# Weights in halves at the start, a store in halves at the end, and a new order between them, in a two-layer attention and feed-forward kernel

**Chip, cores, metric.** One core of one Trainium2 chip. The metric is the device time of one execution in microseconds (us); most quoted times are medians of six executions. The time before is 567.18 us, the median of three executions (565.27 to 567.36).

## The reference, cut to what matters

Four residual steps on x of 2048 x 640: memory attention (four segments of 512 tokens, 32 heads of 20), feed-forward (640 to 1728 to 640), and both again.

```
x = x + A(layernorm(x));  x = x + B(layernorm(x))      # and the same two once more
A: q, k, v = x@wq, x@wk, x@wv                          # 32 heads, width 20
   for s in range(4):                                  # segments of 512 tokens
       p = softmax(q_s k_s' * scale + mask)
       o_s = g * phi(q_s)M / (phi(q_s)z + 1e-6) + (1-g) * p v_s      # g = sigmoid(beta)
       M += phi(k_s)' v_s;  z += sum(phi(k_s))
   out = concat(o) @ wo
B: relu(x @ w1) @ w2
```

## The kernel before

The kernel is a planner. Streams (loads, layernorm, q and k, v, scores, apply, feed-forward, and so on) yield operations, each with the engines that may run it and the buffers that it takes; a table gives every operation a rank, and a list scheduler places them. The result is one fixed order for each engine. Those orders are what runs.

The profile calls TensorE PE, VectorE DVE, ScalarE ACT, GpSimd POOL, and SyncE, which issues transfers, SP. A *chain* of matmuls is a few of them that add up in one bank of PSUM, the memory that matmuls write; another engine must copy the bank out (*evict* it) before the kernel uses it again. The *chain* of the profile is something else: the work that ended last, followed back from wait to wait. A *mode change* is a step between matmuls that use the full array and matmuls on row or column tiles of it.

```
def loads_sp():                              # SyncE's queue
    for i in (0, 2):
        yield from x0("sp", i)               # x tiles 0 and 2, 160 KB each
    yield from ld("sp", "wv", 819200, lambda e: e.dma_start(wv_r[:], w_src(A_wv)), ("wv",))
    ... wk, wq alike
def loads_act():                             # ScalarE's queue
    for i in (1, 3):
        yield from x0("act", i)
    ...
def proj_v(a, s):
    wt = yield Need("wv")
    ...
    for i in range(NJ):                      # 4 x tiles
        for hf in range(2):                  # column halves: one chain of 5 matmuls each
            for k in range(FC): ...          # 128 x 320
...
def store(i):
    r0 = yield Need("xB", b, s, i, 0)
    r1 = yield Need("xB", b, s, i, 1)        # both halves of the last add
    to = yield dma("sp", dout[i], 163840, ...)
```

Ahead of the first v matmul, TensorE runs 14 warming matmuls of 512 columns and some filling ones of 128. Segment 0 then goes: v chains and q and k chains, evictions, scores, exponentials on ScalarE, apply.

The softmax here doesn't subtract the row's maximum and nothing guards it: scores larger than these inputs give would overflow.

Of the kernel before, what the change touches and what calls it, by code (L numbers as in the profile page):

```python
# [11 lines left out]
ALU = mybir.AluOpType  # L12

T = 2048
D = 640
# [399 lines left out]
c-  # L415
n1R3$UbBaqjcK=AZZ6xpVK_yZ5p8?t595eYq@;1$JR!c?v{8kw79EETSf2qA4q(QWdQz<Y6UPL9HYtWYIEZV#TCVR5YmslLBKBtPm=ZQV~UwW!
b&UF6`cC=j-pB`DZR=P0i!~&pF+Fy8Cp0-T!QJd!-~dOIb4cp<XB>@?J?Lk+12nRPfp^Z^36-
UeV1`#rGSypWwAwuExCEu&N@lJfj!m>MChq&ZIo4TS4<CjBJ+U`m|nv8F$Jzbr<H$;q$a!Cv|B_j@29Sz67hLr6b?g2jri0w=8Q-
y0WNiG4>X$ZDBl?{h+x?YBCBc-`6qlIRpw05-;e449SI<)xc{}_d(8W5`jkp?<vgMi8~I|w&43byd&)6a?pD_=%w<a-
YW;>eC%pW{!^!LZx`m;tZ{HGLkBr%tIlI58P@wf@5WeL4uk$MMxV!?a`~b@g8Q%N>yRji>_(*|-  # L420
_aZJYa4#GF*66%A*{>6C&G9IGG2_|b<mvGtD%Qo_*KR1??UHJcF;Bs``U)PdnwC`e)Pm1?0>&p3)}6IJ#q#3z7y|jWvd*N3t*XD@(%3jR?N9w*
2x{<u@|zx8+*J5JNgjxcNlZu4SqMtFUsAxelK=(6=r=zHsJT2Shqp01OMyg98fwecj4FhptT?RJomLjkm?`d4J-
O#@GU_PpIba6PwS#ONc%^yV$R)NApfR&u+xavO0hTCES|uQGii!>nb~auBP~!F0-Xui@?p6K-
eVSN<CS5ojNb{ZKMD<g3u{wIa#&{Nlx~DnZS15C9!*fGgK7@X*o^n}@>y`mWG!|wfwk-KYYo2bl?U!s_}h9=eFA)HSib>&If>cl;{Gu1bwG6ss
LwzXyCB{Bu%d!>LzufBJhsYN?Sfhhv`yxVAc1+sTGB7!eN?w&b_aWJ;ob)B$ziXf@+$O{z`M4Bb4+hYq0<sprSzXBR*!)87&yHIeVaeV;O*oaJ
XtAb=J>YvR?N=jIo$$n*WfXm<PY^{aWBGq0-
qVR?_~X43!ia#C!Argm}lGJmkW0y`e<)%k3z)XahTVmYIkD!W4(_f{g;haIHR}LQ?GzmG{DVfrSO{!+K8~L1$t5$r=r49lWq~3Q8oRnsOc$|`!
O;aXg-4Lt4K?+W?5Cu!foo^d~Z6)>7_C*_FXRcyYShYWplEyM?b?X6^D5yOG3I);2HBXDQGpqu6x&c&{Pucoz-
%<7tvy8)a$}zPYe6l{2J({ytZ#IOLdh@#&uYZ@Ol|CoP)V5n(#WOm)N(BlsIBkY~?VmR)#F&xMO>ofd_T)t4wYs+<i@_@p}lXUWQG~PmjUh%`O
S7^gUhD1+^%Z1!=vNGg*T6-p~d(wm`pvxjp$!_X+)cNqas};eJdfQDKLzh@J_gTc$7kSSLZ%RxRsE9i_ZEuN_Z<l75AL5e-  # L430
<;_L+l|r(^Sa8tYrm>$gS!^EU9SM=&oVl^iF~@qCx%4<re8bcIi+)J%`_DQ&K@V5QKC_mCX2N8!B1!N1*4IVJPRhP^R=Z@WCJy%{c0&%!zF-
;bonB__w7kN0)!cd()^=pbTrj<|C0oJ0l9SjvUZxgc{c5fMWi&cEMHGT`}Hpq~|IBO)C?K8Ep9Sf@Hf8ed|@H$SO{`F3}S7BY=B3jJvCp8o!tg
`T2;y~e?UCV?_?BwSr8ex;1NZa{Wd_)tPVt%9m6?A3dh26R6-?gr+&fid?}#`>?A5g-
c@B_iJN6vwEE>VU5dA!FE_^##`w<9WjPGaGE?<QH%!#oT`MPKr3~BSv4oI`tHT&b&se_8P6yKvbLnhZxZc(R3bKtiLIu#;f$vw^_U@{zn6vU(K
m+MSGPBy9{dEBaCQO{&F}ijy|}g=0T+pzk6$H!DmxwHUctjQh%>$CFsG?w*I8X#U3L>vYc@wLd>osE=`3o$830!{CCJ=r!kt4hw3upltrr)>&+
TV;PVpXX@_{&+hr5fESj1R*cmX5zN(IK&D$=O*F#+JuQ{!T$Q47PO4#$VdXFw+2MMT@Lqy3aX&L-
2&m`eI$E0s7Kd*Oi{UXoCB4{r$V)~UaaLbR>#}uRKb-
m0TGzZRHFX!3!&H9y9v8Oh0x?B;3E3(L4dfIVe|DMg<svI4?=}sg*f~AGW`t@lMnG$+u6mo^n9xjYUj4yrKClQPMUCS_S=)Z><T#+*zqeuUq*Z
PWP%rk~UmzXclhPY>T8j%-t9ak@CDRA=|j=9p?U^zr3&+%)>u#F($Qa}b3*f|SX%V*k@+-3`HCBY_++1_i!<SK>J?xUx_TM2l|5qa3!Qt-
)T)LO^j+b3}~gIcMJ`bPDA@{qm)uQxg`0%tDj_jSFzUmjCK1Ygyo`g8J>-YI{AN=Ws;^dTV8am@NPxnJk>S^YhE0=%BXno-nFcgx51wEn654)p  # L440
9$jXc1!G_OAZDn8AeKc~+C<(Gqg%|8}_Tuy7x1I`AFIOxSOHE|9;pVu>*2mSTVX~ffaT7Aw_jf%{4R{iNXixc*GutOE=hOje_kUnzkI%ci&SQA
g<H0(hoWfemmuM%R3;r}-3vK!?mh$%DB(<~yjMVGhXuGMfgyjyr>j6FGC4ZNpfL;J(Hw-xg<R4YFtpL88mEL&KoSaoPs(#x)i&ni|9qgENF9N%
-7U_}Fz%iuQzYIS*jZk+M5MGTvSeMYO|jbk)3zvznh>2iSr1~Xa`GEtd1cqN>cQqa4N-b5sj(~s-H23GZ&MbZIO;sVmJc#?z@*o)gqxT-
LcdKpUL<YfbSBf*|`NK(Z9nE2DOcn`Uq2~pgmlRj>b0yekU)F}{7{Y|+eCGCILi+H`L`->QPexR5H{F8=V`Bm)!DqcI0^rM-tHWKD=7siqTcU9
sV>A3+U=vW0NMXi>HeC08$=Q35qIWM7~TMbcUN#hXXmvshynBmM>RJzBllQdxEtU&J>z0_9@GeK{0K<14%<>#N^Oqa;F#EwhPyZUiGE9~<)xb@
|agO$^OC@mwVq+~I<#5@qO7WTAi)ZGd!I#kqAQP8d{>d8Ki_>9|06crOMd+(~P!d$)%@fu#ztk{|P>j~{+WYa{o$O`jnCv`#lo^Kj{Y|f&Vga6
+y*UNj5|98u;%H3FJU6?E78o2_pd}1+|<9a!CavC(hO}&~7Ejg-
=vB_iU8hkUB@2aouO)Fh|e_bO+7xVG|!TV9IvWL=wm8_5QTWY<g68P)`x3YXpV|E~F>{w;IZc^XZ$Q_t>J$UUwgqy?;ty5z$wG&RR>C!ZQ5cmH
AQEd-&vRl0uR+-
T&j55oRp~}eBmA#PR@8Txr)@A!jj(Bwh(JPZ{xu2>$sYmn?%4eOiR4$FIpEV=LR?HF?GM?J~CUJH`>$Wj_2FUils3x00_eU$^lwpXS!;~GtRK|  # L450
&XwqWj7yw^u-*e5)`QbA;{GlotuI=rTvC1<y!0V)UZedMI-SxMbp(RI<T=x^M?`I5X<OYGS==<P6O{wDM`&f0VbyKld(W+Cen9T4k<K14g!Fyo
+1L@n?hlEctto0*_a6qYmg+BrWY&%lm*vCEsII{P&n)v9|tg)QvCDwI0>t4_a*aZ(Rq)y}8^FB+C}S)(16e^JxC_sdkOtS&cz+X2kq99884(Av
-Q<fQj$*0;{8X>AhoE&$ixkE|a$CY$t_?w~h$+vc=DgVr+L?Zn!nu!D8k?xnno0i*S5CVx&1>)wdb=YfA??m2}vy7Enp>6;nG_RAMEWkk0w=*#
-JTA!<f>sfi%tDjGH$DfKGjJ_NlaHH<+b0+l@#L8EY+djN6k_YLbb$W^AkTSGnC*@YguL@&JD^z@jpRaV5OU^ReWZ;|9+kc>+#_9ZPZ7`O1#Ln
MF#()no7L4%zFe~UG+T-cSu?t|`>l28jR;5`d?{}#IZ|4g8cH5XEu5s3dEb+{)5TQ-
7=lBWiswTfdAFndc)#zc5Qjc}Ug*IjPXa0+*FlO2NTrb~ZH1E<zlXJ`3aMpR5W$)q^%&E(zq3?7X`;&&r*MYuawOc@Ml4rOMpU#-
^NANw4S5tPfub2@fKTa)LCK!f)T#T!K)f>RGi`PE(+-t-iWxP!GF>oHn7$Q%!9U5!O<;cHwPOXc34(RS<*EM1XKMVb+Q8`~eDc3<aHQ27k4ps-
WW-z{oQqE$YsKx#D?qQ6XpWMe-K1J)ACT7^hZ$pv;pftiWXU`s{SuMYH?$cN`#QyP6h}jWOO&1#bAY-DTz8ujz3OTlh_XF_!wbWc5D(HyyvsGq
y(K^$Ng0I5^;?Uul*Si>BtP5S1R=}W5)?XGcCZRcdn$ZMh-
?y`Kx!+yMPI*R+?vxJEM$E|ZF`TCotJGG=f*zB#<yYjxw95)`a3+<2dM!qu0mmC5T^ZV}QI=XjDmhN^ZO~j595%AE?CS!H`6q#4FM}?-  # L460
JR|Rb7x~WcY3z6Qv~|J8*}I+x9zOx}`3CBO9Y6r*VdOQ}V)nfd9Bqe(To>_Z7}}e~^@#kfi`ZX32NG|FTpw^}^aa!p9|WgKNbwZrw;{_GBHFqv
VNQb@9D+V_`NCWe>C_999|aV#5^C~Z_thhxG$5F0pabXYKSM)LI_u0gafZ_Zw=HQ@pvg4ggpH{B##o=_MJ<>PbPp_w7(#df2;HzxuUFT@L6gu=
Z}u^G<|g)}Ew`+J{)Sk2WdYfgLs!FAA9A)LFQl%q$6X0N)8sts{?}xIUD`H%Bw-
!rv6`L0@qp1)A9HW+E=KSISM*);kZr~oZ)|ioeaR79_ABI`6>f3ys_srybXuc;-
~HX;FrE%n^EuIH6guTGW9&n2K}VsJobhL{S01nGrX57gjs|M<IN<31?z|M@;!yYYDu@MW`-
uL0$X53LOMNHT_7Py29pdefcAmI7DL8!&{@20v9L6mIO++R5Wm~@Ls&X$p`qvTX4<V!eue02Hz5JD{AgZmAkGr~j241|*jqzE}?Z;K8LG`Fscp
8tPu3rQC$JKY7U*+=(+q*rpxQ56s2gM^RXVk6gfczQWmqL=Yp}U$f|HZ(YksL=>wdnpf-mQuu&MKt5#bp8i<jhfLUCO9qr`0+YUuIviArHDNWd
0#o5b-~%Fj{w6!CoRib{T7kj1?w4d2UJ!Yo&YwXJ~Z-8oUry@j6zvP0Y#gYZ;N_GF1EfC~KARe-
<;x5Ft{mIjbFfE@D=f^1iOyKyOhk!k^MEJMZfef7f7^Jz=#~Q;>U1#wlH0UPLU|4ysqk57{;7Ad8&B%r3pIgn3(W?xw^#5!<2tG3H~~2lRH3(j
?>=2OnR@b%+(Z>`~8R&bUkyr>w=^c4Phq>}ee+Zv>Y$SUG~ZqZl3H{#uZzLrU9Vaf|zHXm>%+WhS3MoL<l8-  # L470
&3Hv0R9d3Ypok#v2PtUGs`~5PVk=Q6PYQZvT68n7b{2Tm4^{m%gp0lR(C7<9z^r)(C09pI5%;B98xVpzT=43Cv`1%UE;_xb~OtA)8uFLruc+o6
# [63 lines left out]
def bass_interleave_layers__memory_aug_infini_attn__dense_activation_relu__prompt_kernel(  # L535
    nc, A_x, A_wq, A_wk, A_wv, A_wo, A_beta, B_x, B_w1, B_w2, out,
):
    with contextlib.ExitStack() as es:
# [3 lines left out]
        def sem_(name):  # L542
            if name not in sems:
                sems[name] = es.enter_context(nc.semaphore(name))
            return sems[name]


        NWARM = 14
        APART, JOINT = [[0], [1], [2], [3]], [[0, 1, 2, 3]]
        LN2_APART = (0, 7)  # L550

# [1163 lines left out]
```

## Time and profile before

| quantity | before |
|---|---|
| TensorE busy | 556.4 of 563.8 us |
| first v matmul starts | 9.48 us |
| first exponential on ScalarE starts | 19.50 us |
| last matmul starts | 560.71 us |

In the profile a row is start, duration, engine, line, operation, output and input, with the idle time of the engine before it in brackets. This is ScalarE around the first exponentials (`PT<-ps`), from the timeline of the kernel before:

```profile
18.36 0.60 ACT L939 ACTIVATE wb<-ps 128x512 bf16<-128x512 f32 x1 [0.48 <-PE ps L951]
18.85 0.22 ACT L787 ACTIVATE gt<-beta_bc 128x32 f32<-128x32 bf16 x1
19.10 0.23 ACT L788 ACTIVATE gt<-gt 128x32 f32<-128x32 f32 x1
19.50 1.94 ACT L1304 ACTIVATE PT<-ps 128x1024 bf16<-128x1024 f32 x2 [0.17 <-PE ps L1290]
21.32 0.77 ACT L796 ACTIVATE va<-gt 128x128 bf16<-128x128 f32 x1
```

And this is the busy time by stretch (stretch, its length, then PE, PEld, DVE, ACT, POOL with instruction counts, granted clock, DMA share, GB/s):

```profile
20.00:25.00 5.00, 5.00 (x39) 2.13 (x38) 5.00 (x15) 4.95 (x7) 4.41 (x9) 1.00 0.19 43
25.00:30.00 5.00, 4.95 (x33) 1.96 (x32) 4.41 (x16) 4.84 (x7) 4.09 (x10) 1.00 0.68 193
30.00:35.00 5.00, 5.00 (x61) 2.77 (x57) 4.84 (x12) 4.64 (x7) 2.43 (x5) 1.00 0.48 134
```

From the first exponential on, TensorE is full and ScalarE is 93 to 99% busy; VectorE, at 88 to 100%, is hardly less so. TensorE cannot run ahead there by much: the scores need PSUM that the exponentials must first empty.

### The profile page before, as it was taken

The page shows a single profiled execution, that of the slowest core. Times are in us where ns is not written, and L with a number is a line of the kernel's source. Part 1 is how long each engine was busy: PE and PEld are TensorE (multiplying, and loading weights), DVE is VectorE, ACT ScalarE, POOL GpSimd, SP SyncE. Part 2 cuts the span into 40 slices and gives each one's busy share as a digit, 9 for nine tenths or more (in the row PEclk, how much of TensorE's full clock was granted, in tenths as well). Part 3 has the DMA queues.
Part 4 walks back from the last instruction along what each step waited for, and adds up shares of the span by engine and source line. Part 5 has one row for each costly group of instructions (what it writes and reads, how often), then busy time and mean ns, then how long its engine had stood idle before and what let it go on. Part 6 is the DMA issues. An engine that isn't in the chain of part 4 may idle for free.

```text
span 563.8 us, 12521 instructions
## 1 busy us (share of the span) xinstructions
PE 556.4 (99%) x5115; PEld 297.7 (53%) x5118; DVE 420.9 (75%) x1024; ACT 422.5 (75%) x517; POOL 214.9 (38%) x341
## 2 busy tenths in 40 slices
PE   8999999999999999999999999999999999999997
PEld 5454455445555445644546454565545654755655
DVE  6789989998998878857689956998778876424202
ACT  3899999999889878688897978878898778023140
POOL 3664546454454343452345433244333443002000
PEclk9999999999999999999999999999999999999999
DMA  6435787776534343573255451565116531431201
GB/s 221 129 90 133 152 145 150 226 153 106 90 70 85 57 72 62 81 119 76 44 82 106 80 84 20 96 124 93 33 19 91 99 82 20 86 73 36 59 1 47
DMA packets 126609, 50.62 MB, mean 90 GB/s; under 512 B 112120, under 2 KB 124600, under 8 KB 126552
## 3 DMA queue, kind: packets, MB, share of 16 engines
q1 hardware_dynamic: 124568, 42.19, 40.3%
q0 software_dynamic: 1552, 7.29, 4.5%
q8 instruction: 40, 0.66, 0.5%
q10 hardware_dynamic: 432, 0.34, 0.2%
q14 instruction: 17, 0.14, 0.1%
HBM read 15.16 MB, written 7.37 MB: 40 GB/s over the span
## 4 chain that ended last, share of the span: by engine, by line
PE 91%; DVE 5%; ACT 2%; DMA 1%; issue 0%; SPq 0%
PE ps L1590 21%; PE ps L1620 20%; PE ps L951 15%; PE ps L1290 9%; PE ps L998 8%; PE ps L1536 7%; PE ps L1372 7%; DMA wv_r<-in_A_wv_dram 1%; PE ps L1153 1%; PE ps L1240 1%; ACT PT L1304 1%; DVE x_sb L1478 1%; PE ps L1602 1%; DVE stats L868 1%; DVE stats L869 1%; PE ps L1096 1%
## 5 line engine op out<-in xcount | busy, mean ns | idle before, releaser
L1304 ACT ACTIVATE PT<-ps 128x1024 bf16<-128x1024 f32 x256 | 248.3, 1024 | 42.9 <-PE ps L1290 42.1
L1280 POOL TENSOR_SCALAR_AFFINE_SELECT PT<-PT 128x512 bf16<-128x512 bf16 x256 | 173.1, 692 | 235.8 <-ACT PT L1304 195.5
L1620 PE MATMUL ps<-wb,hT 128*128 128x320 bf16 x896 | 133.0, 300 | 0.1
L1590 PE MATMUL ps<-xnT,wb 128*128 128x512 bf16 x520 | 127.4, 380 | 0.0
L1478 DVE TENSOR_TENSOR x_sb<-x_sb,ps 128x320 bf16<-128x320 bf16 x128 | 60.7, 479 | 73.3 <-PE ps L1620 49.5
L1620 PEld LDWEIGHTS ps<-wb,hT 128*128 128x128 bf16 x896 | 84.2, 98 | 37.5 <-issue 5.9
L1572 ACT ACTIVATE hT<-ps 128x512 bf16<-128x512 f32 (+1 forms) x65 | 37.4, 577 | 54.5 <-PE ps L1590 53.9
L1590 PEld LDWEIGHTS ps<-xnT,wb 128*128 128x128 bf16 x520 | 47.2, 98 | 54.8 <-issue 7.6
L1301 ACT ACTIVATE PT<-ps 128x1024 bf16<-128x1024 f32 x64 | 62.1, 1024 | 12.2 <-PE ps L1290 12.0
L998 PE MATMUL ps<-wv_r,xnT 128*128 128x320 bf16 x320 | 57.0, 300 | 0.9 <-DMA wv_r<-in_A_wv_dram 0.8
L951 PE MATMUL ps<-xnT,wq_p 128*128 128x512 bf16 x200 | 55.8, 380 | 0.1
L951 PE MATMUL ps<-xnT,wk_p 128*128 128x512 bf16 x200 | 54.9, 380 | 0.0
L1536 PE MATMUL ps<-wo_r,oT 128*128 128x320 bf16 x280 | 50.2, 300 | 0.0
L1571 DVE TENSOR_SCALAR hT<-ps 128x512 bf16<-128x512 f32 (+1 forms) x47 | 31.9, 680 | 12.9 <-PE ps L1590 12.6
L1372 PE MATMUL ps<-PT,va 128*32 128x128 bf16 (+3 forms) x896 | 40.8, 302 | 0.0
L998 PEld LDWEIGHTS ps<-wv_r,xnT 128*128 128x128 bf16 x320 | 29.6, 98 | 20.8 <-issue 2.6
L938 DVE CAST kq<-ps 128x512 bf16<-128x512 f32 x43 | 29.4, 683 | 10.0 <-PE ps L951 9.6
L1290 PE MATMUL ps<-kq 20*128 20x512 bf16 (+3 forms) x560 | 35.3, 301 | 1.2 <-ACT PT L1304 1.2
L1536 PEld LDWEIGHTS ps<-wo_r,oT 128*128 128x128 bf16 x280 | 26.8, 98 | 15.5 <-issue 2.0
L881 DVE TENSOR_SCALAR xn_tok<-x_sb,mv,rstd 128x640 bf16<-128x640 bf16 x64 | 30.0, 482 | 3.2 <-POOL rstd L877 3.1
L868 DVE BATCH_NORM_STATS2 stats<-x_sb 128x6 f32<-128x320 bf16 x64 | 30.1, 471 | 1.6 <-DMA x_sb<-in_A_x_dram 1.4
L1372 PEld LDWEIGHTS ps<-PT,va 128*32 128x32 bf16 x896 | 18.9, 96 | 21.9 <-issue 11.0
(112 smaller groups left out, 620.7 us busy)
## 6 DMA issues: line engine op xcount, KB each, us to landing
kq_scr<-kq SPq DMA_DIRECT2D x28, 120.0 KB
kqL<-kq_scr SPq DMA_DIRECT2D x28, 120.0 KB
out_dram<-x_sb SPq DMA_DIRECT2D x16, 160.0 KB, 2.0
wb<-in_B_w_dram POOLq DMA_DIRECT2D x5, 432.0 KB, 4.2
x_sb<-in_A_x_dram POOLq DMA_DIRECT2D x3, 640.0 KB, 5.3
wb<-in_B_w_dram POOLq DMA_DIRECT2D x2, 640.0 KB, 5.8
kq_away<-hT SPq DMA_DIRECT2D x5, 256.0 KB, 4.8
kq<-kq_away SPq DMA_DIRECT2D x5, 256.0 KB, 5.1
```

Source lines behind the costliest of these rows:

```text
L951: fn = lambda e, bank, k=k, w_p=w_p, c=c: e.matmul(bank, w_p[:, k, c * 128:(c + 1) * 128], xnT[:, k_, :, k, :], start=(k == 0), stop=(k == ...
L998: fn = lambda e, bank, k=k, i=i, hf=hf: e.matmul(bank[:, 0:320], xnT[:, k_, i, k, :], wv_r[:, k, hf * 320:(hf + 1) * 320], start=(k == 0), ...
L1280: tm = yield pool(590.0, lambda e: e.affine_select(out=reg, in_=reg, pattern=[[0, 4], [1, 128]], compare_op=ALU.is_ge, fill=0.0, base=0, c ...
L1290: fns.append((lambda e, x=x, j=j, hh=hh, N=N, o=o: e.matmul(ps[:, hh, o:o + N], kq(b, gg[x], 0)[32 * hh:32 * hh + DH, 128 * j:128 * j + 12 ...
L1301: fn = lambda e: e.activation(PT[:, :, 2 * k:2 * k + 2, 1024:1280], bs.ap.rearrange("p h (x t) -> p x h t", x=2), ACT.Exp, scale=SCALE)
L1304: fn = lambda e: e.activation(PT[:, items[0], 2 * k:2 * k + 2, c0:c0 + 512], bs.ap, ACT.Exp, scale=SCALE)
L1372: return [(lambda e, hh=hh, j=j: e.matmul(bank[32 * hh:32 * hh + 32, 128 * j:L], v_flat[b][:, (j * H + 8 * hh + g) * E1:(j * H + 8 * hh + ...
L1478: ta = yield dve(320, 1, lambda e: e.tensor_tensor(xa, xa, bk.ap[:, 0:320], ALU.add), [tk], early=HOT)
L1536: fn = lambda e, bank, k=k, hf=hf, o=ot.ap: e.matmul(bank[:, 0:320], o[:, k, :], wo_r[:, k, hf * 320:(hf + 1) * 320], start=(k == 0), stop ...
L1572: lambda e: e.activation(d, bk.ap[:, 0:n], ACT.Relu), [tk] + hs[0].old + (hs[1].old if dc >= NSTG // L else []))
L1590: fn = lambda e, bank, k=k, dc=dc: e.matmul(bank, w1_r[:, k, dc * 128:(dc + 1) * 128], xnT[:, k_, :, k, :], start=(k == 0), stop=(k == FC ...
L1620: fn = lambda e, bank, dc=dc, q=q, h=h, hf=hf: e.matmul(bank[:, 0:320], h, w2_r[:, q, hf * 320:(hf + 1) * 320], start=(dc == 0), stop=(dc ...
```

## The change

It is meant to start the matmul stream earlier, to take air out of it, and to shorten what follows the last matmul.

```diff
-                for i in (0, 2):
-                    yield from x0("sp", i)
-                yield from ld("sp", "wv", 819200, lambda e: e.dma_start(wv_r[:], w_src(A_wv)), ("wv",))
+                yield from x0("sp", 0)
+                for hf in range(WV_PARTS):
+                    c0, c1 = D * hf // WV_PARTS, D * (hf + 1) // WV_PARTS
+                    yield from ld("sp", "wv%d" % hf, 819200 // WV_PARTS, lambda e, c0=c0, c1=c1: e.dma_start(
+                        wv_r[:, :, c0:c1], w_src(A_wv)[:, :, c0:c1]), ("wv", hf), lat=(3300.0, 4300.0)[hf])
...
-                for i in (1, 3):
+                for i in (1, 2, 3):                          # ScalarE's queue takes x tile 2
...
-                    tu = yield pool(300.0, ...LN_EPS...)
+                    tu = yield Op([("pool", ...)] + [("dve", ...)] * EPS_DVE, aggr)
...
+                        if a * NSEG + s in V_FREE:           # segment 0: each v chain a stream of its own
+                            S.spawn(chain(i, hf), "v0")
...
+                    if s == NSEG - 1 and i == NJ - 1:        # last tile
+                        for hf in range(2):
+                            S.spawn(store_half(i, hf), "store")
+                        return
...
 TABLE = """                                                 # all ranks new
```

(A paired form of apply stays switched off.)

## The prediction

> **What bounds the kernel now.** I read the page's engine table first, then the chain that ended last, then the waits of the TensorE, and at last the timelines of the first 16 and last 14 us, since the change names the two ends of the kernel.
>
> The engine table and the clock row of the page:
>
> ```profile
> PE 556.4 (99%) x5115; PEld 297.7 (53%) x5118; DVE 420.9 (75%) x1024; ACT 422.5 (75%) x517; POOL 214.9 (38%) x341
> PEclk9999999999999999999999999999999999999999
> ```
>
> The PE has 563.8 - 556.4 = 7.4 us without a matmul, at full granted clock. The chain of work that ended last says the same by its shares:
>
> ```profile
> PE 91%; DVE 5%; ACT 2%; DMA 1%; issue 0%; SPq 0%
> ```
>
> So this is one nearly unbroken stream of matmuls, whose count the change leaves alone (the pairing of applies comes switched off). Only three things can move: when the stream starts, how much air is in it, and what follows its last matmul. The start, from the chain in order of time (start, duration, what):
>
> ```profile
> 1.72 7.62 DMA wv_r<-in_A_wv_dram
> 9.48 0.43 PE ps L998 x2
> 9.91 0.28 PE ps L845 x5
> 10.19 1.36 PE ps L998 x10
> ```
>
> The stream starts at 9.48 us, when the v weights have landed (9.35). What precedes it on the PE are warming matmuls and transposes of x. The waits of the PE over the whole run (total us, times, longest us):
>
> ```profile
> PE ps L820 <- DVE ktok L817: 1.2, 1, 1.2
> PE ps L1290 <- ACT PT L1304: 1.2, 2, 0.8
> PE ps L998 <- DMA wv_r<-in_A_wv_dram: 0.8, 1, 0.8
> PE ps L1240 <- DVE o_sb L1229: 0.4, 1, 0.4
> ```
>
> A reader may take 0.8 us as all that the v weights cost. The timeline corrects this: how soon x tile 0 could have been ready counts too. Its rows for that tile:
>
> ```profile
> 3.77 0.49 DVE L868 BATCH_NORM_STATS2 stats<-x_sb 128x6 f32<-128x320 bf16 x1 [1.35 <-DMA x_sb<-in_A_x_dram]
> 4.97 0.19 DVE L870 BATCH_NORM_AGGREGATE mv<-stats 128x2 f32<-128x12 f32 x1
> 5.25 0.23 POOL L875 TENSOR_SCALAR lnU<-mv 128x1 f32<-128x1 f32 x1 [3.53 <-DVE mv L870]
> 5.56 0.57 POOL L877 TENSOR_TENSOR rstd<-lnU,nhalf 128x1 f32<-128x1 f32 x1
> 7.32 0.75 DVE L881 TENSOR_SCALAR xn_tok<-x_sb,mv,rstd 128x640 bf16<-128x640 bf16 x2
> 8.26 1.30 ACT L853 ACTIVATE xnT<-ps 128x640 bf16<-128x640 bf16 x2 [5.25 <-PE ps L845]
> ```
>
> The scale of tile 0 is ready at 6.13, but VectorE does statistics of other tiles first and normalizes at 7.32. With v weights at 9.35 that cost nothing. With earlier weights it would. The end, from the timeline:
>
> ```profile
> 550.16 11.74 SPq L1580 DMA_DIRECT2D out_dram<-x_sb  x4
> 561.05 0.49 DVE L1478 TENSOR_TENSOR x_sb<-x_sb,ps 128x320 bf16<-128x320 bf16 x1 [1.41 <-PE ps L1620]
> ```
>
> The last add ends at 561.54, the last of the four stores is issued at 561.57 and lands at 563.35 (read from the trace's semaphore events), and the span ends at 563.84.
>
> **What the Trainium skill says.** (1) "Perfetto Trace Analysis", Identifying the Most-Contended Engine: matmul busy time is a poor measure, because matmuls are pipelined. The trace agrees: a 320-column matmul is listed at 300 ns, but 112 of them run in 15.33 us in the last stage, 137 ns each. I therefore measured air by start-to-start times, less columns/2.4 GHz. (2) "TensorEngine Tiling (Array Packing)", Key Properties: changing the tiling mode drains the TensorE. By those start times, going from full array to row tiles costs a median of 99 ns, row tiles to full 263, full to column tiles 96, back 139, row to column 131. There are about 400 such changes, some 45 us, by far most of the air. (3) "DMA: Bandwidth & Descriptors", Why small descriptors are slow: about 3 cycles of overhead per packet beside bytes/32. Halving rows from 1280 to 640 bytes means 2*(20+3) = 46 against 43, an estimate of 7% more engine time. This trace has no 640-byte packets; the 1280-byte ones take 55 ns, 1024-byte ones (other sources and targets) 64 ns. (4) The same page, Why a DMA increments its semaphore by 16 and not by 1: a load is there only when the slowest of its engines has finished. The trace shows this strongly: the sixteen increments for the v weights came from 6.53 to 9.35 us, ten of them by 6.91. Size alone does not set the landing.
>
> **The change part by part.**
>
> Start, the weights. The v load is 800 KB. Landings of the three weights at 9.35, 11.55 and 13.60 mean 2.1 to 2.2 us per 800 KB. The first half, 400 KB, now has one x tile ahead of it in its queue instead of two, and is issued about 0.45 us sooner. Taking off half the bytes (1.1 us) and 0.45 us: 9.35 - 1.55 = 7.8 us. If the lag of the slow engines (2.4 us) shrinks with the size too, 1.2 us more: 6.6. I take 7.2. The second half should land near the old time, about 9.0 to 9.5, and k and q weights where they did, up to 0.2 us later.
>
> Start, x tile 0. If its chain goes first: statistics at 3.77 (0.41 + 0.40), aggregate to about 4.75, epsilon on VectorE (the change allows that) to 4.9, the power on GpSimd 0.57 plus a hand-over, to 5.6, normalization 0.40 to 6.05, five transposes 0.46 to 6.5, eviction 0.65 to 7.2. So the first v matmul starts at 7.3 at best. I take 7.6, as the later of weights and tile with some slack: **1.9 us** earlier than 9.48.
>
> What is lost again there. A v half chain is 5 x 136 = 0.68 us. Tile 1 follows tile 0 by VectorE's pace, 0.81 + 0.12 + 0.40 = about 1.35 us, so near 8.9, and the second weight half is about as late. From 7.6 + 0.68 = 8.3 to 8.9 the PE is short of work; the free order of chains is there to keep that gap small. After it, 7 chains (4.8 us) and three sets of transposes (0.9 us) last to about 14.6, and the k weights come at 11.6, so nothing more runs dry. Loss 0.5 us, net **1.4 us**. Before, from 9.48 on the PE was busy without a break (5.00 of 5.00 us in the stretch 10 to 15), so work brought forward there shortens the stream.
>
> End. The store of 128 rows of 1280 bytes has its packets in about 0.5 us, half of it in 0.25; the rest of the 1.8 us is fixed. The first half goes out 1.9 us earlier, at the previous add (559.15 + 0.49), clear of the second. **0.2 us**.
>
> Middle, the new order. By start times, waits beyond the usual cost of each transition, without the first 10 us, sum to about 3.8 us. The largest are 0.85 at 158.6, 0.39 and 0.23 just after, 0.48 at 72.9, and ten of 0.1 to 0.3. 19 of the 64 applies start from full mode instead of following a row round; each one joined would save about 96 + 139 + 99 + 263 - (99 + 131 + 139) = 228 ns, 4.3 us in all. A search by stretches may get some of both: I credit half of the waits (1.8) and two or three of the joins (0.5), less 0.3 for new waits where the model it was found with errs: **2.0 us**.
>
> Sum: 1.4 + 0.2 + 2.0 = **3.6 us**. The runs of before are 565.27, 567.36 and 567.18, and the profiled one 565.58: mean 566.3. 566.3 - 3.6 = 562.7; from the median it would be 563.6. I say **563.0 us**.
>
> **The rivals.**
> A, the halves don't come sooner: twice as many descriptors of half the size take their turns on the same engines, the slow ones set the landing, and the first half lands at 8.5 to 9. For it: in the trace the engines' share of DMA is 0.99 from 5 to 10 us, so bytes moved earlier push others back. Against: they are the first bytes in their queue. Then the start gives 0.3 us, and the time is 564.2.
> B, another wait takes over. From 139 to 160 us the chain runs mostly through VectorE (dense there with evictions, statistics and adds), and ScalarE is busy 57.8 of the 60 us from 60 to 120. A start gained on the PE survives only if these streams shift with it; if their first work is tied to the q weights (13.6 us), the PE waits near 158 us instead. For it: the PE's greatest wait in the middle is exactly there. Against: the new order was chosen with this in the model, and the tail from 480 us on is PE work alone, which other stretches can lend from. Then 1 to 2 us remain: 565.
> C, the order finds more: most waits and a dozen joins. Then 2 + 0.2 + 5.5 = 8 us: 558.5. Against: the kernel is already tuned, and all but 19 applies are joined.
> D, the order was fitted to a model that errs on the chip: 1 to 3 us of new waits; 566 to 568.
>
> **Range and chances.** A, B and D raise the time to 564 to 567, C lowers it to 559; 561 to 565 is the core. The runs of one kernel scatter by 2 us. So 560.5 to 565.8 for 8 in 10. Faster by over 2% needs less than 555.8, which is 11 us: more than all the waits and joins together with the start; 2%. Slower by over 2% needs 11 us of new air: 1%.
>
> **What would show it.** Right: first L998 matmul at 7.3 to 8.2 us; first half of v landed by 7.8; the chain begins with x tile 0 and VectorE instead of the v load; the last add to the end of the span 2.1 us instead of 2.3; summed waits in the middle 1.5 to 3 us, mode changes within 5 of before. Wrong: first L998 after 8.8 (A); PE waits over 1 us between 139 and 160 (B); far fewer mode changes (C); more waits than before (D). The whole prediction fails if the number of matmuls differs or the granted clock is not full.

## The result, and the profile after

After: **565.79 us** median of six (565.32 to 566.67); before, in the same rounds: 567.0 (565.2 to 567.36). The ratio is 0.9988, 95% interval 0.997 to 1.0006: the same. A ratio here is the mean time of one kernel's fast runs over that of the other's in the same rounds, so not quite the ratio of the medians. The 3.6 us were not found.

The engine table and the chain's shares, after:

```profile
PE 556.5 (99%) x5114; PEld 296.5 (53%) x5114; DVE 422.7 (75%) x1040; ACT 426.3 (76%) x519; POOL 208.2 (37%) x323
PE 90%; DVE 6%; ACT 3%; DMA 1%; issue 0%; POOL 0%
```

TensorE's busy time is what it was. The start of the chain, after (start, duration, what):

```profile
0.80 3.04 DMA x_sb<-in_A_x_dram
...
6.50 0.31 DVE xn_tok L889
...
6.88 0.44 PE ps L853 x5
7.32 0.89 PE ps L787 x16
8.21 0.48 PE ps L1004 x3
```

The v load is off the chain; x tile 0 and VectorE have its place, as the prediction wanted. The first v matmul (line 1004) starts at 8.12 us instead of 9.48. The halves of v landed at 5.70 and 7.49 us (semaphore events of the trace). So the tile gates the start, and not the weights: VectorE takes statistics of another tile before it aggregates those of tile 0 (5.06), and more of them before it normalizes tile 0 at 6.42, as its timeline shows:

```profile
4.67 0.48 DVE L876 BATCH_NORM_STATS2 stats<-x_sb 128x6 f32<-128x320 bf16 x1
5.06 0.19 DVE L878 BATCH_NORM_AGGREGATE mv<-stats 128x2 f32<-128x12 f32 x1
5.17 0.44 DVE L876 BATCH_NORM_STATS2 stats<-x_sb 128x6 f32<-128x320 bf16 x1
5.52 0.87 DVE L877 BATCH_NORM_STATS2 stats<-x_sb 128x6 f32<-128x320 bf16 x2
6.31 0.19 DVE L878 BATCH_NORM_AGGREGATE mv<-stats 128x2 f32<-128x12 f32 x1
6.42 0.39 DVE L889 TENSOR_SCALAR xn_tok<-x_sb,mv,rstd 128x640 bf16<-128x640 bf16 x1
```

TensorE's waits, after (total us, times, longest; cut: 1.2 for the warming operand as before, and one of 0.2):

```profile
PE ps L853 <- DVE lnU L883: 0.7, 1, 0.7
PE ps L853 <- DVE kqL L1100: 0.6, 1, 0.6
PE ps L1311 <- ACT PT L1325: 0.5, 1, 0.5
PE ps L1681 <- DVE x_sb L1527: 0.4, 1, 0.4
PE ps L1496 <- DVE va L993: 0.4, 1, 0.4
```

The wait for v weights (0.8) is gone; in its place TensorE waits 0.7 us for tile 0 ahead of its first transposes (the profile names the operation just behind the normalization). The two of the scores for `PT` (1.2 in all, at 158 and 73 us) have become one of 0.5 us, at 21.4 us. New are also the transposes' wait for a bank that VectorE must empty (at 32.1 us) and two more for VectorE. The wait at 21.4 us ends with an exponential of ScalarE, whose timeline after reads:

```profile
18.30 0.60 ACT L947 ACTIVATE wb<-ps 128x512 bf16<-128x512 f32 x1 [0.37 <-PE ps L959]
18.79 0.22 ACT L796 ACTIVATE gt<-gt 128x32 f32<-128x32 f32 x1
19.04 0.80 ACT L804 ACTIVATE wb<-gt 128x128 bf16<-128x128 f32 x1
19.32 1.08 ACT L804 ACTIVATE va<-gt 128x128 bf16<-128x128 f32 x1
19.91 2.26 ACT L1325 ACTIVATE PT<-ps 128x1024 bf16<-128x1024 f32 x2
```

Two copies of the gate (line 804), which the order before has on GpSimd, now stand ahead of the first exponential. It starts at 19.91 us, later than before (19.50), although everything up to the first v matmul was 1.4 us earlier. The copies are only part of this. TensorE itself comes to the first scores no earlier, as its rows show:

```profile
10.75 3.19 PE L1004 MATMUL ps<-wv_r,xnT 128*128 128x320 bf16 x22
13.78 1.24 PE L959 MATMUL ps<-xnT,wk_p 128*128 128x512 bf16 x5
19.09 0.39 PE L1311 MATMUL ps<-wb 20*128 20x512 bf16 x4
```

The scores start at 19.09 us, in the kernel before at 19.07. Between the first v matmul and them the new order has 40 matmuls of v, 11 of k and 15 transposes, the old one 34, 10 and 10 (counted in the traces), with under 0.4 us of air in either. The time gained is spent on work that the old order does later.

How far is one kernel ahead of the other at a given time? Summed matmul work done by then puts the changed kernel ahead by about 1.0 us from 10 to 18 us, and level at 33. (Work is columns / 2.4 per ns: in the trace matmuls of 128, 320 and 512 columns start 56, 136 and 216 ns apart, so 192 columns more take 80 ns.) At the end, too, they are level: the last matmul starts at 560.65 us, against 560.71.

The end, after:

```profile
559.61 2.23 SPq L1628 DMA_DIRECT2D out_dram<-x_sb  x2
560.99 0.49 DVE L1527 TENSOR_TENSOR x_sb<-x_sb,ps 128x320 bf16<-128x320 bf16 x1 [1.42 <-PE ps L1681]
```

The last add ends at 561.48, the last half is issued at 561.51 and lands at 563.09; the span ends at 563.59. That is 2.11 us from the add to the end, against 2.30.

### The profile page after: what moved, and what is told of

Same layout as the page of the kernel before. It is cut to its first block, busy times and chain, and to the rows that moved or that the text cites. A ratio compares the mean times of both kernels' runs of the same rounds, so it can differ in the third digit from the quotient of the medians.

```text
span 563.6 us, 12517 instructions
## 1 busy us (share of the span) xinstructions
PE 556.5 (99%) x5114; PEld 296.5 (53%) x5114; DVE 422.7 (75%) x1040; ACT 426.3 (76%) x519; POOL 208.2 (37%) x323
## 4 chain that ended last, share of the span: by engine, by line
PE 90%; DVE 6%; ACT 3%; DMA 1%; issue 0%; POOL 0%
PE ps L1681 21%; PE ps L1651 20%; PE ps L959 14%; PE ps L1311 8%; PE ps L1585 8%; PE ps L1004 7%; PE ps L1393 7%; PE ps L1261 1%; ACT PT L1325 1%; PE ps L1174 1%; PE ps L1663 1%; DVE stats L877 1%; PE ps L853 1%; DVE stats L876 1%; DMA x_sb<-in_A_x_dram 1%; DVE hT L1620 1%
## 5 line engine op out<-in xcount | busy, mean ns | idle before, releaser
L1681 PE MATMUL ps<-wb,hT 128*128 128x320 bf16 x896 | 134.5, 299 | 0.4 <-DVE x_sb L1527 0.4
L1621 ACT ACTIVATE hT<-ps 128x512 bf16<-128x512 f32 (+1 forms) x69 | 39.7, 577 | 55.4 <-PE ps L1651 54.8
L1004 PE MATMUL ps<-wv_r,xnT 128*128 128x320 bf16 x320 | 58.2, 300 | 0.0
L959 PE MATMUL ps<-xnT,wq_p 128*128 128x512 bf16 x200 | 54.4, 380 | 0.0
L1004 PEld LDWEIGHTS ps<-wv_r,xnT 128*128 128x128 bf16 x320 | 29.3, 98 | 18.4 <-issue 2.8
L1620 DVE TENSOR_SCALAR hT<-ps 128x512 bf16<-128x512 f32 (+1 forms) x43 | 29.2, 678 | 11.9 <-PE ps L1651 11.6
```

The costliest lines, as they stand in the source:

```text
L959: fn = lambda e, bank, k=k, w_p=w_p, c=c: e.matmul(bank, w_p[:, k, c * 128:(c + 1) * 128], xnT[:, k_, :, k, :], start=(k == 0), stop=(k == ...
L1004: fn = lambda e, bank, k=k, i=i, hf=hf: e.matmul(bank[:, 0:320], xnT[:, k_, i, k, :], wv_r[:, k, hf * 320:(hf + 1) * 320], start=(k == 0), ...
L1621: lambda e: e.activation(d, bk.ap[:, 0:n], ACT.Relu), [tk] + hs[0].old + (hs[1].old if dc >= NSTG // L else []))
L1681: fn = lambda e, bank, dc=dc, q=q, h=h, hf=hf: e.matmul(bank[:, 0:320], h, w2_r[:, q, hf * 320:(hf + 1) * 320], start=(dc == 0), stop=(dc ...
```

## The experiments

Two things on the way in which they are read. First, an **order that is replayed**: in each kernel below (a_again apart) the planner takes a recorded list of operations in place of the ranks, so that one part of an order can be exchanged and the rest kept. before_again checks the method. (The lines of these kernels are numbered anew; in the rows shown 935 and 894 are warming and filling, 1066 is q and k, 1111 v, 960 the transposes of x, 1432 the exponentials, 1788 the second feed-forward matmul.) Second, **measures**. Whole times scatter by more than most effects, so three starts are read from each profile: first v matmul, first exponential, last matmul. Waits beyond the usual cost of a transition and the cost of mode changes are summed over the start-to-start times of the matmuls, as in the prediction. For scale, a_again and e4_oldload repeat the changed order: 552.47 and 552.52 us from first v to last matmul, against 552.53 in the first profile. This measure is good to 0.06 us among kernels that start alike.

| run | first v | first exp. | last matmul | all median | full-clock mean | at 0.997 |
|---|---|---|---|---|---|---|
| kernel before (66 in six batches) | 9.48 | 19.50 | 560.71 | 565.50 | 565.42 | 18 |
| changed kernel | 8.12 | 19.91 | 560.65 | 565.79 | 565.85 | 0 of 6 |
| a_again | 8.43 | 20.23 | 560.90 | 565.93 | 565.85 | 0 of 6 |
| before_again | 9.27 | 19.30 | 560.57 | 565.46 | 565.48 | 0 of 4 |
| e1_end | 8.95 | 18.97 | 560.50 | 565.31 | 565.16 | 2 of 6 |
| e3_graft | 8.58 | 19.64 | 560.72 | 565.63 | 565.68 | 1 of 6 |
| e4_oldload | 8.38 | 20.21 | 560.90 | 566.31 | 566.32 | 0 of 6 |
| e2_loads | 11.04 | 22.73 | 564.02 | 568.79 | 567.25 | 3 of 6 |
| e7_late | 10.48 | 20.50 | 561.74 | 566.40 | 566.62 | 0 of 4 |
| e8_tight | 7.57 | 25.16 | 566.25 | 572.97 | 571.36 | 3 of 5 |
| e9_tight | 7.63 | 18.38 | 559.72 | 564.89 | 564.76 | 1 of 6 |
| e10_gt | 8.78 | 20.18 | 560.50 | 565.02 | 565.09 | 0 of 6 |
| e11_warm | 9.68 | 19.70 | 561.07 | 565.94 | 565.83 | 2 of 6 |
| e12_cold | 9.27 | 19.28 | 560.68 | 565.46 | 565.37 | 2 of 6 |
| e13_both | 7.78 | 18.46 | 560.22 | 565.17 | 565.11 | 0 of 6 |
| e14_wait | 9.33 | 19.36 | 560.92 | 566.22 | 565.78 | 2 of 6 |
| e15_late | 8.84 | 20.64 | 561.37 | 566.00 | 565.94 | 0 of 6 |
| e16_early | 8.11 | 19.29 | 559.97 | 565.33 | 565.37 | 0 of 6 |
| e17_best | 8.79 | 19.48 | 560.33 | 564.23 | 564.37 | 0 of 6 |

"Full-clock mean" is the mean of the executions whose listed granted clock is 1.0; "at 0.997" counts those listed there (e2_loads had a fourth at 0.994; three executions, one each of e9_tight, e15_late and the kernel before, are at 0.999 and in neither column). Before took 566.75 to 567.49 us at 0.997, mean 567.21.

### The changed kernel again, and its parts one at a time

**a_again**: the changed kernel, five more rounds.

> The changed kernel once more, so that the variants have it on the same chip in the same rounds. Both theories: 0.6 us (0.1%) under before, with a second profile to see which of the waits at 21, 32, 66 and 161 us come back.

565.93 us, ratio 1.0003 (0.9988 to 1.0017). The 0.6 us that I still expected are not there. At full clock the changed kernel is about 0.4 us *longer* (565.85 against 565.42). The 0.9988 of the first call came from its company: four of the six executions of before were at 566.8 us or more.

**before_again**: the kernel before, replayed.

> Before itself again, its instructions in the same order on every engine, for a second profile of it. Expected by both theories: the waits after the first v matmul come back at the same places and with the same lengths (0.85 at 158, 0.48 at 73, 0.38 at 159 us); the landing of the v weights differs from 9.35 us. If the profiled execution is one of those near 567.2 us, it shows where the 1.9 us are.

565.46 us, ratio 0.9996 (0.9979 to 1.0012), the same waits at the same places. Replaying costs nothing.

**e1_end**: the kernel before with the last tile stored in halves.

```diff
-order: ... add(last tile, half 0), add(last tile, half 1), store(last tile)
+order: ... add(last tile, half 0), store(half 0), add(last tile, half 1), store(half 1)
```

> Before, in exactly its own order on every engine, with nothing but the last output tile stored in halves. Both theories: the matmul stream as in before, the span 0.25 us shorter at its end (last add to end of span 2.05 us where before has 2.30); in time 0.2 to 0.3 us, hardly to be told from noise.

565.31 us; full-clock mean 565.16, which is 0.26 under before's, and from last matmul to end of span 2.9 us instead of 3.1. The end is worth what was predicted.

**e3_graft**: the new loads and the changed order up to its first k matmul (13.8 us), before's order from there, whole store.

```diff
-order: changed[0:]
+order: changed[:132] + [op for op in before if op not in changed[:132]]
```

> Before's order from about 13.7 us on, with the changed kernel's loads and its order of the first 13.7 us; the last tile stored whole. Theory 1 (the new order after the start gives the gain back): first v matmul at 8.1 us, before's later order keeps the lead of 1.0 us, so 1.0 to 1.3 us under before (566.5 to 565.3). Theory 2 (from about 20 us on ScalarE and VectorE set the pace in any order, so a start gained on TensorE is absorbed): the lead is gone by 35 to 160 us, the time within 0.3 us of before.

565.63 us (full-clock mean 565.68). The stream starts 0.7 us before that of before_again, and the last matmul is no earlier (560.72 against 560.57). The two new waits of 0.32 and 0.23 us at 20 to 21 us take most of it, and 0.27 us is a set of transposes that merely changed sides of the first v matmul. So **the gain at the start is lost again within 3 us of the first exponential, even with the order before behind it** (by summed work it is 0.35 us ahead of before_again from 14 to 18 us, and level at 22). The first scores start at 19.20 us, in before_again at 18.87: the graft holds the new order's v work ahead of them, 39 matmuls and 15 transposes against 34 and 10. In before_again five of these v matmuls run from 19.78 us; in e3_graft they are done by then, and the two waits stand in their place. From first v to last matmul it takes 552.14 us, 0.39 *less* than the changed order with the same start: the new order between the ends is a loss.

**e4_oldload**: the changed order with v loaded whole behind two x tiles.

```diff
-loads_sp: x0, wv half 0, wv half 1, wk, wq      loads_act: x1, x2, x3
+loads_sp: x0, x2, wv, wk, wq                    loads_act: x1, x3
```

> The changed kernel's order and its last store in halves, but the v weights loaded whole behind two x tiles as before. Theory 1: first v matmul at about 9.4 us, and that 1.3 us goes through to the end: 1.3 us over the changed kernel, 0.7 us over before. Theory 2: the late start is absorbed in the waits at 21 and 32 us: within 0.3 us of the changed kernel.

566.31 us (565.58 to 566.94), ratio 1.001. In its profile v had landed whole by 7.85 us and the first v matmul still came at 8.38, behind the eviction of tile 0. The 9.35 us of the first profile was a late one: in the seven profiles with v whole behind two x tiles the first of the load's sixteen increments came at 6.4 to 6.8 us, the last at 9.35, 9.13, 8.88, 8.82, 8.37, 7.85 and 7.65. The profiled execution, with the weights at 7.85, was the fastest of its six, so it does not show what late weights cost in this order. The means say 0.47 us (566.32 against 565.85 for the changed kernel), between the 1.3 and the 0.3 us of the two theories.

**e2_loads**: before's order, only the loads changed.

```diff
-loads_sp: x0, x2, wv, wk, wq                    loads_act: x1, x3
+loads_sp: x0, wv half 0, wv half 1, wk, wq      loads_act: x1, x2, x3
```

> Before's order on every engine and its store, with nothing but the loads changed: v weights in halves behind the first x tile, x tile 2 on the other queue. Theory A (before, in its profile, waited for one slow engine of the v load; in other executions the weights come before x tile 0 is turned): weights landed by 7.9 us, first v matmul set by tile 0's eviction at 8.8 to 9.0 us, as in the run with only the end changed; so the load part alone brings 0 to 0.1 us on the usual execution. Theory B (the late v load is usual, and is also what makes the executions near 567.2 us): first v matmul 0.5 us or more earlier than before's 9.48, and no execution above 566.5 us.

568.79 us, ratio 1.005 (1.0032 to 1.0069): slower by half a per cent. The third tile on ScalarE's queue landed at 7.41 us, and VectorE, which takes its list in order, stood before that tile's statistics with tile 0 behind them. TensorE idled 2.44 us ahead of its first transposes, and its clock fell. The windows:

```profile
8.00:10.00 2.00, 0.21 (x4) 0.21 (x5) 2.00 (x8) 0.00 (x0) 1.20 (x4) 1.00 1.07 374
10.00:12.00 2.00, 1.65 (x21) 1.32 (x19) 1.01 (x3) 1.30 (x2) 1.81 (x4) 0.85 0.58 197
12.00:14.00 2.00, 2.00 (x9) 1.16 (x8) 1.26 (x5) 0.70 (x1) 1.00 (x1) 0.50 0.00 0
14.00:16.00 2.00, 2.00 (x17) 1.47 (x16) 0.60 (x3) 1.62 (x5) 0.00 (x0) 0.79 0.68 182
```

The clock column falls to 0.85, 0.50 and 0.79, together (0.15 + 0.50 + 0.21) x 2 us / 0.5 = 3.4 us at half clock. This execution is listed at 0.997. New loads need a new order of VectorE; with the new one (e3_graft) the same loads bring no such idle time.

**e7_late**: before's order, v loaded behind k.

```diff
-loads_sp: x0, x2, wv, wk, wq
+loads_sp: x0, x2, wk, wv, wq
```

> Before's order and store, with the v weights loaded whole behind the k weights, so that they land some 2.2 us later than usual (10 to 11.5 us). If a late start goes through one to one to the end: time 1.2 to 2.5 us over before's fast executions. If ScalarE and VectorE set the pace from 20 us on: under 0.5 us over them.

566.4 us, ratio 1.0016. First v 1.21 us later than in before_again, first exponential 1.20 later, last matmul 1.17 later. A *later* start goes through in full. An earlier one, as e3_graft showed, does not.

**e8_tight**: tile 0 straight through its layernorm, all v chains, then before's order.

> New loads, last tile in halves, before's order from about 13.7 us on, and in the first 13.7 us x tile 0 taken straight through: its two statistics, aggregate, epsilon on VectorE, one other tile's statistics while GpSimd takes the power, then its normalization. Expected first v matmul at 7.4 to 7.7 us. If a start gained goes through: last matmul at 559.8 us, span 562.5, time 1.0 us under before's fast executions. If it is absorbed by 35 us: last matmul at 560.4 or later, time within 0.4 us of the run with only the end changed.

572.97 us, ratio 1.0121. This kernel was flawed: my coding of the buffers sent every one of the first v chains into the same PSUM bank, and TensorE waited 0.7 to 1.1 us between each two. It tells only that the first v matmul can start at 7.57 us.

### What sets the end

In the runs with before's order, at least from the first exponentials on, the last matmul starts 541.1 to 541.5 us after the first *exponential*: 541.21, 541.27, 541.53, 541.24 in before, before_again, e1_end, e7_late, 541.29 and 541.09 in e2_loads and e8_tight, whose first v matmuls are 3.5 us apart (and 541.08 in e3_graft).

**e9_tight**: e8 made right, with the banks chosen as they come free.

```diff
-order: before                       # v chains, k and q chains, scores by before's order
+order: tile 0 aggregated, scaled, normalized ahead of the statistics of tiles 2 and 3;
+       v chains of tiles 0 to 2; k and q chains as soon as their weights are permuted; then before
```

> The flawed e8_tight made right: x tile 0 is taken straight through its layernorm, the first v chains follow on the halves, each chain takes whichever PSUM bank is free, and from there the order is that of the kernel before, with the last tile stored in halves. Theory F (what sets the end is when ScalarE's first exponential starts, because ScalarE is 95 to 97% busy from 20 to 130 us; in six runs with the before order the last matmul started 541.1 to 541.5 us after it): the first v matmul comes at 7.5 to 7.7 us, the first exponential at 18.3 to 18.8 us (18.97 at the earliest so far), and the last matmul 541.1 to 541.5 us after that, at 559.5 to 560.2 us; time 563.9 to 564.9 us. Rival G (what sets the end is when the first v matmul starts, 551.2 to 551.6 us before the last matmul in the before order): last matmul at 558.8 to 559.2 us, time 563.3 to 563.8 us. Rival H (nothing at the start matters): time within 0.2 us of the kernel before with the store in halves, 565.2 us. No wait of over 0.4 us between the first v chains this time.

564.89 us, ratio 0.9987 (0.997 to 1.0005); full-clock mean 564.76. First v at 7.63, first exponential at 18.38, last matmul at 559.72: 541.34 after the exponential, as expected, and 552.09 after the first v matmul, where the rival had 551.2 to 551.6. It has 34 v matmuls ahead of the first scores, as before. The first exponential, from the timeline:

```profile
18.24 0.23 ACT L903 ACTIVATE gt<-gt 128x32 f32<-128x32 f32 x1
18.38 1.93 ACT L1432 ACTIVATE PT<-ps 128x1024 bf16<-128x1024 f32 x2
```

**e10_gt**: the changed kernel with the gate copies where before has them.

```diff
-ScalarE: gate, copy(v buffer 0), copy(v buffer 1), exp, exp    GpSimd: copy(v buffer 2)
+ScalarE: gate, exp, exp, copy(v buffer 2)                      GpSimd: copy(v buffer 0), copy(v buffer 1)
```

> The changed kernel with one thing put back: the three copies of the gate into the v tiles are on the engines of the kernel before (two on GpSimd, the third on ScalarE behind the first two exponentials) instead of two on ScalarE ahead of the first exponential (0.80 and 1.08 us there). Theory A (waits of TensorE add up): the first exponential starts at 19.2 to 19.5 us instead of 19.9 to 20.2, the scores' wait of 0.54 us at 21.4 us goes to under 0.2 us, the later waits stay, and the last matmul starts 0.3 to 0.5 us sooner after the first v matmul than 552.5 us; time 565.2 us. Rival B (the stretch from 20 to 40 us is tied down by VectorE, 5.00 of 5 us busy at 30 to 35): the wait of 0.70 us at 32.1 us grows by what is saved, and the time stays at 565.6 to 565.9 us.

565.02 us, against 565.79 and 565.93 of the changed kernel. In the profile the scores' wait is gone, and the one for `kqL` stayed what it was:

```profile
PE ps L960 <- DVE kqL L1207: 0.6, 1, 0.6
PE ps L1788 <- DVE x_sb L1634: 0.4, 1, 0.4
```

From first v to last matmul: 551.72 us instead of 552.53. Apart from these three copies the traces show the same order on every engine. Two copies on the wrong engine cost 0.8 us of the stream, and without them the new order is 0.42 us better than before's with the same start (552.14). The expected absolute starts were missed (20.18 us, not 19.2 to 19.5), because the profiled execution began late, for the reason told under e17_best. From first v to first exponential it is 11.40 us, against 11.79 in the changed kernel and 10.02 before: the copies are 0.4 us of that difference, the work ahead of the scores the rest.

**e13_both**: the start of e9_tight up to the second exponential, then the order of e10_gt.

> The start of e9_tight up to the second exponential, then the order of e10_gt (the changed kernel with the gate copies put back), store in halves. Theory F (the end is set by when the first exponential starts, plus a length that belongs to the order that follows): e9_tight had its first exponential at 18.38 us, and in e10_gt the last matmul started 540.3 us after the first exponential (541.3 in e9_tight, 540.7 in the changed kernel), so the last matmul starts at 558.5 to 559.1 us and the time is 563.2 to 563.8 us, all executions at a granted clock of 1.0. Rival I (gains at the start and in the order do not add, because the wait of 0.70 us at 32 us takes up whatever lead TensorE has): last matmul at 559.6 to 560.4 us, time 564.4 to 565.2 us.

565.17 us (full-clock mean 565.11), last matmul 560.22: the rival's figure. The first exponential was at 18.46, but 541.76 us passed from there to the last matmul, not 540.3. The wait for `kqL` at 32 us was still 0.70 us, and one of 0.72 us at 28.9 had joined it. (In its profile the halves of v landed late, at 7.27 and 8.41 us; its first v matmul came at 7.78 all the same.) So "first exponential plus a length of the order" holds for before's order, over first exponentials from 18.4 to 25.2 us, and *not* in general.

### Where in the middle, and the best version

**e15_late** and **e16_early** divide the two orders at some 150 us, with the same start.

```diff
 e15_late:  order: changed up to 150 us + the rest as before
 e16_early: order: changed start + before up to 150 us + the rest as changed
```

> The changed kernel up to some 150 us, from there the order of the kernel before (its loads, its store in halves, all else as changed). It divides the two orders in time. So far 13 of 48 executions of the kernel before were at a listed clock of 0.997, and none of 30 with the changed order. Theory E (the cause lies in the stretch from 150 us on, where the order before keeps TensorE busy 1.00 of 2 us at 158 to 160): some of the six executions are at 0.997 and 1.6 to 2 us longer (by the share of the kernel before one or two; none has a chance of 0.15), the others at 565.3 to 566.2 us. Rival D2 (the cause lies ahead of 150 us): all six at 1.0.

> The counterpart: the order of the kernel before from 14 us to some 150 us (the start as in e3_graft), from there the changed order. Theory E: all six executions at 1.0, 565.3 to 566.3 us. Rival D2 (the cause lies ahead of 150 us): one or two of six at 0.997 and 567 us or more. If neither of the two shows an execution at 0.997, or both do, the place stays open.

From first v to last matmul: 552.53 us for e15_late, 551.86 for e16_early, beside 552.53 (changed throughout) and 552.14 (e3_graft, before throughout). The changed order loses ahead of 150 us (552.53 against 551.86, with the same end) and behind before's first part it gains 0.28 us (552.14 to 551.86). Behind its own first part it gains nothing (552.53 both times). In e16_early the bunch of waits at 158 to 160 us (0.85, 0.38, 0.23, 0.17) has become one of 0.59, 0.23 and 0.12.

**e17_best**: the start of e9_tight, before's order up to 150 us, the changed order from there, store in halves.

> The start of e9_tight and the order of the kernel before up to some 150 us, from there the changed order, store in halves: the pieces that the runs showed to be the shortest. Theory (the pieces are independent once the stretch from 20 to 40 us is the same): e9_tight's last matmul at 559.7 us, less 0.3 us that the changed order saves from 150 us on (551.86 us from first v matmul to last in e16_early against 552.14 in e3_graft), makes 559.2 to 559.6 us and a time of 564.1 to 564.6 us, under the kernel before at full clock (565.4 us, 40 executions) and the changed kernel (565.85 us, 12 executions). Rival (as with e13_both, a wait takes the gain back): last matmul at 559.7 to 560.2 us, time 564.7 to 565.2 us.

**564.23 us** (563.79 to 565.02), ratio **0.9964** (0.9947 to 0.998): the only run whose interval lies wholly below 1 and the best version found, 1.05 us under before by the full-clock means (564.37 against 565.42). The time met its range. The profile missed it (last matmul 560.33, expected 559.2 to 559.6): it fell on an execution of 565.0 us that began late. What holds such an execution back is seen in the rows of the warming matmuls, of the changed kernel and of e17_best:

```profile
1.25 4.59 PE L828 MATMUL ps<-ktok 128*128 128x512 bf16 x14 [1.25 <-DVE ktok L825]
```

```profile
1.25 6.13 PE L935 MATMUL ps<-ktok 128*128 128x512 bf16 x14 [1.25 <-DVE ktok L932]
7.20 0.52 PE L894 MATMUL ps<-ident 128*128 128x128 bf16 x6
7.55 0.44 PE L960 MATMUL ps<-ident,xn_tok 128*128 128x128 bf16 x5
```

The same 14 matmuls take 4.59 or 6.13 us. By their starts they are 427 ns apart at first and 216 later; the step came 2.9 us after the first of them in the changed kernel's profile and not within 5.5 us in e17_best's. The warming is then still running when tile 0 is normalized (6.01), and its transposes wait till 7.55. With v weights that land at 8.4 us or later much of the delay is hidden, with early ones not. This agrees with the Trainium skill, "TensorE: Matmul & The Clock Gate", Part 1: The HAM clock gate, which says that the array runs at half clock until a free-running window of about 3.4 us has been busy. I read this from the profiles; no run was made for it.

### The executions at 0.997

18 of 66 listed executions of before ran at a mean clock of 0.997 and took 1.8 us longer (567.21 against 565.42). A share of 0.3% is 1.7 us lost, or 3.4 us at half clock: as much as e2_loads shows openly at 10 to 16 us. No profile caught such an execution of before itself, so this is inferred. The changed kernel had none in 12.

**e11_warm** and **e12_cold**: before with 14 filling matmuls more, or without its 26.

```diff
 e11_warm: order: ... transposes of tile 1, +fill 14, first v chain
 e12_cold: order: ... -fill 23, transposes of tile 0, -fill 3, transposes of tile 1, first v chain
```

> The kernel before with one addition: 14 more filling matmuls (128 x 128, some 0.75 us by the 23 that took 1.45 us) behind the transposes of x tile 1, where TensorE waited 0.81 us for the v weights. Theory C (the executions of the kernel before at 567.2 to 567.4 us, listed with a granted clock of 0.997, are those in which the idle time ahead of the first v matmul let the clock drop for some 3.4 us): all six executions are listed at 1.0 and lie between 565.2 and 566.1 us; where the weights land early the fill costs up to 0.4 us. Rival D (they have another cause): some of the six are listed at 0.997 and take 567 us or more, as 8 of 28 of the kernel before did.

> The kernel before with one thing taken away: its 26 filling matmuls ahead of the first v matmul (1.45 us and 0.33 us), so that TensorE idles for some 1.5 us more before 8 us. Theory C (idle time of TensorE ahead of the first v matmul lets the clock drop): most or all of the six executions are listed with a granted clock of 0.997 or below and take 566.9 to 567.5 us, and the profile shows a granted clock under 1.0 somewhere between 8 and 16 us. Rival D (it has another cause): no more than a third of the executions are at 0.997, as in the kernel before, and the others take 565.2 to 565.6 us.

Both had 2 of 6 at 0.997, about the share that before has (18 of 66). The idle time just ahead of the first v matmul, 0.8 us or twice that, is not the cause, and my theory fell. (e11_warm costs 0.4 us at full clock, e12_cold nothing: the filling matmuls do nothing here.)

**e14_wait**: before with one pair swapped on ScalarE at 157 us, to lengthen TensorE's wait.

```diff
-ScalarE: exp(scores), exp(scores), exp(keys)
+ScalarE: exp(keys), exp(scores), exp(scores)
```

> The kernel before with one pair swapped at 157 us: ScalarE takes its exponential of the keys (1.06 us) before the two exponentials of the scores (1.94 us) instead of behind them, so that TensorE's wait of 0.85 us at 158.4 us becomes some 1.4 to 2.4 us. Theory E (the executions of the kernel before at 0.997, 10 of 33, come from the stretch at 158 to 160.5 us, where TensorE is busy 1.00 of 2 us because waits of 0.85, 0.38, 0.23 and 0.17 us lie together; the changed kernel is busy 1.7 of 2 us there, and it and its two relatives with the same order had 0 of 24 executions at 0.997): most or all of the executions are at 0.997 and 1.6 to 2 us longer than the wait alone makes them (566.0 to 566.6 us alone, 567.8 to 568.6 us with it), and if the profile is of such an execution its granted clock is below 1.0 between 158 and 166 us. Rival D (a cause elsewhere): a third of the executions at most are at 0.997, as before; time 566.0 to 566.6 us for the others.

The wait grew by 0.24 us only (0.85 to 1.09), less than it needed to; 2 of 6 at 0.997. This decides nothing. e15_late and e16_early were also to tell: neither showed an execution at 0.997. Added up, kernels with the changed order from 150 us on had 0 of 42, before itself 18 of 66, and the replayed kernels with before's order from there 10 of 50 (e2_loads and e8_tight left out). That leans towards the stretch behind 150 us, but e15_late's 0 of 6 does not support it. **The cause stays open.**

## Why the prediction was wrong, point by point

**End: right.** 0.2 us was predicted; e1_end gives 0.26 at full clock, and the interval from last add to end of span is 2.11 instead of 2.30 us.

**Start: the mechanism right, the size off, and the step after it wrong.** The halves came earlier than predicted (5.4 to 5.9 and 7.3 to 7.9 us in nine of eleven profiles, 6.3 and 7.9 in e2_loads, 7.3 and 8.4 in e13_both, not 7.2 and 9.0 to 9.5). Tile 0 became the gate, and the first v matmul came at 8.12 where 7.3 to 8.2 was said (8.43 in a_again). The 7.6 us that were taken assume tile 0 straight through its layernorm, which the changed order does not do; e9_tight does, and has 7.63. And 9.48, from which the 1.9 us were counted, was an execution with a late load; other profiles of before's loads and order have 8.95 to 9.33. The step that failed is "work brought forward there shortens the stream", backed by TensorE being 5.00 of 5.00 us busy from 10 to 15 us. TensorE was busy there, but from 20 us on it shares the bound with ScalarE and VectorE, and what matters is when it comes to the first scores. The new order fills the time gained with v work: first scores at 19.09 us, as before (19.07), first exponential at 19.91, later. The v work brought forward is then missing at 20 to 22 us, and TensorE waits there. e3_graft shows it: first v 0.7 us earlier, first exponential 0.3 us later, last matmul not earlier. In the main this is rival B, which the prediction looked for at 158 us on the strength of 57.8 of 60 us ScalarE; it acts at 20 to 33 us, where ScalarE is as full. B's tie to the q weights is not what held: they landed at 11.91 us after, and q's first matmuls follow the v chains without a wait. To keep the gain the first exponential must come sooner too, as in e9_tight (18.38 us). Which engine limits at 20 to 33 us is not separated: of e3_graft's two waits the longer (0.32 us) is for an eviction by VectorE, the other for ScalarE, and the one of the changed kernel at 32 us is for VectorE.

**Middle: the failed step is the 2.0 us.** "I credit half of the waits (1.8) and two or three of the joins (0.5), less 0.3": it was a credit without evidence. The order in fact costs 0.39 us (552.53 against 552.14 with the same start). By its terms: summed waits 4.47 us against 3.85 in e3_graft, 0.6 more instead of 1.8 less; mode changes 398 against 399 and 57.20 us against 57.44, 0.24 less instead of 0.5. (What counts as the usual cost of a change moves each of these sums by some 0.2 us; the 0.39 us is read directly. The prediction's "some 45 us" for all changes was too small: summed as here they cost 57 us.) This is rival D, smaller than the 1 to 3 us that it named. Its largest single item is named by e10_gt: two copies of the gate ahead of the first exponential, 0.8 us. Without these the order is a gain of 0.42 us, still a fifth of what was credited.

**Base.** The mean of before over all batches is 565.9 us (predicted base 566.3). It mixes two kinds of execution, 565.42 and 567.21 us. The changed kernel lies above the first and well below the second, so a mean gain of under 0.1 us hides a loss of 0.4 us at full clock.

Sum at full clock: end -0.26, middle +0.39, start and join +0.3 (e3_graft's 565.68 less 565.42), together +0.4, as measured (565.85 less 565.42). Of the signs named for "wrong", "more waits than before" is the one that came true. The time, 565.79 us, lay just inside the range; the gain that was forecast did not come.

## What to carry to other kernels

A full engine does not make its start the lever: look which other engine is nearly full just behind it, ask when *that* one gets its first work, and count what the order puts ahead of it. A new order found on a model should be taken apart on the chip by swapping its stretches one at a time; here the best kernel found is a tightened start, then before's order up to 150 us and the new one behind it. And sort the executions by their listed clock: the first ratio measured how many slow ones the other kernel had.

## What the Trainium skill lacked or had wrong

- "TensorE: Matmul & The Clock Gate", Part 1: The HAM clock gate. It gives about 4 us, give or take 500 ns, for the rise to full clock. Its matmul spacings agree with the runs (427 and 216 ns at 512 columns). The spread was larger here, 2.9 us to over 5.5 us after the first warming matmul; a later note of the same part, by which one kernel had 6, 11 or 14 slow matmuls, fits the runs better. The profile's clock row reads 1.00 all this time.
- The same page has an idle window of about 3.4 us as the cause of a drop. In e2_loads the longest idle gap was 2.44 us, and 3.4 us at half clock followed. No page gives a length of short idles that would account for the 18 of 66 executions at 0.997 of a kernel whose longest wait, once TensorE has begun, is 0.85 us; adding or removing some 0.8 us of idle time at the start changed nothing.
- "TensorEngine Tiling (Array Packing)", Key Properties, says that a change of mode drains the array, with no cost. Medians here: full to row tiles 99 ns, row to full 264, full to column 96, column to full 139, row to column 131; in all 57.2 to 57.5 us of some 551, in 398 to 400 changes.
- "DMA: Bandwidth & Descriptors", Why small descriptors are slow. Its overhead gave an estimate of 7% for halving rows of 1280 bytes. Packets of 640 bytes took a median of 32 ns in the changed kernel, those of 1280 bytes 55 to 58 (profiles of before, after and a_again): 10 to 16%.
- The same page, Why a DMA increments its semaphore by 16 and not by 1, has the slowest engine decide, without a size. For one 800 KB load the last increment came at 7.65 to 9.35 us in seven profiles, the first at 6.4 to 6.8 each time.
